# Some twenty operations of a written order change places: cosformer attention with a feed-forward network on one core

## The chip, the core and the metric

The kernel runs on one core of a Trainium2 chip. A core has five engines with a queue of instructions each: TensorE (PE, the matrix products), VectorE (DVE), ScalarE (ACT), GpSimd (POOL) and SyncE (SP), which here only starts DMA transfers. An engine takes its instructions strictly in the order of its queue; between engines semaphores tell that an operand is ready or a buffer is free. The metric is the device time of one execution in microseconds (us), lower is better.

## The reference

Queries, keys and values have 8 batches, 8 heads, 576 positions and 64 columns. The attention has no softmax: relu(q) and relu(k) are multiplied by the cosine and the sine of the position, which gives 128 features each, and so a 128x64 matrix per head takes the place of the matrix of scores.

```python
q_p = concat(relu(q) * cos, relu(q) * sin)      # k_p likewise
kv  = einsum('bhsf,bhsd->bhfd', k_p, v)
z   = sum(k_p, axis=2)
x   = einsum('bhsf,bhfd->bhsd', q_p, kv) / (einsum('bhsf,bhf->bhs', q_p, z) + 1e-06)
h   = x.reshape(4608, 512) @ w_in               # 512 x 2048
g   = maximum(0.01 * h, h)
out = g @ w_out                                 # 2048 x 512, float32
```

## The kernel before

**Groups.** The 4608 rows of x are cut into nine groups of 512 rows. Groups 0 to 7 are the first 512 positions of a batch; group 8 gathers the last 64 positions of all eight. For each batch the features of k are made (nine slices j of 64 positions), then the sum kv over all 576 positions. For each group the features of q are made and transposed by a DMA; numerator and denominator are products with kv on TensorE; DVE divides (`xs`); x is transposed by a DMA (`xT`), and the two products of the feed-forward network follow.

**Products as seven block products.** The first product from group 3 on and the second from group 1 on are cut into 2x2 blocks and each is worked out with seven block products in place of eight, at the price of sums of blocks, which run on DVE and POOL.

**The order is written by hand.** A string, `PROGRAM` (line 25 on), holds 1126 calls such as `k_sin(2,7,D)`; lines 1192 and 1193 parse it and run each call, and every engine executes its instructions in the order in which these calls emit them. Nothing reorders them later, and the waits between engines follow from the data. A call that stands earlier in the string is thus earlier only in the queues of the engines on which it puts instructions. The last letter of an argument list names the engine: D is DVE, A is ACT, P is POOL. The calls that matter here:

- `k_cos(b,j,engine)`, `k_sin(b,j,engine)`: one half of the features of slice j of batch b, a single instruction (line 395 on ACT, line 397 on DVE and POOL) from the staged `kst` into the tile `kp`, of which there is one: a new batch's k operations wait for the kv sum of the batch ahead.
- `kv_sum(b,...)`: 72 small matmuls (line 472) that read the whole `kp` and the values `vm`, and a copy on ACT (line 479).
- `num(b,j)`: 8 matmuls (line 559), and on DVE denominator, reciprocal and product (lines 570, 574, 575) into `xs`.
- `q_prep(b,j,engine)`: two instructions (line 395 or 397) into `qp`; `q_transpose_dma` and `x_transpose_dma` put one DMA each on SP's queue (line 523 for x); `x_sum(b,n,engine)` adds blocks of `xT` into `X` (line 686).
- `M(g,m)`: 128 columns of the first product for all rows of group 1 or 2 (line 633), after each second one a leaky relu on ACT (line 644). After m=15 it also emits two sums of blocks of `g` on DVE.
- `P(g,u,n)`: a block product of the first matrix in groups from 3 on, 4 matmuls of 256 columns (line 786) into one of four PSUM banks `ps_f`. Each unit u uses three banks A, E, B_. `e(g,u,x)` are the operations between them: b copies A to B_, s copies E to `s5`, u copies B_ to `u1` (on ACT, line 403; written as capitals on DVE, line 405), y adds `s5` to B_, z adds `u1` to E (DVE), and a, c, d, e are the leaky relus of the finished blocks (ACT, line 813). P(g,u,7) accumulates onto B_, and so waits until u has copied it.
- `F(g,i)`: 4 matmuls of a block product of the second matrix (line 903) into a bank `ps`; `g_sum(g,n,...)` forms the sums of blocks that products 3, 5 and 6 read (line 686 on DVE). Finished blocks are combined on DVE (line 686) or copied by ACT (lines 922, 931).

Names: `kp<-kst,sin_t` is a k operation, `ext<-g` and `ext<-ext,g` are sums of g, `osb` is a piece of the output on its way to memory, `w_` and `T` are sums of weights.

Of the kernel before, what the change touches and what calls it, by code (L numbers as in the profile page):

```python
# [52 lines left out]
F(1,8) k_sin(3,0,P) k_sin(3,4,P) k_cos(3,0,A) k_cos(3,3,P) k_sin(3,5,D) k_cos(3,5,P) num(2,0)  # L53
q_prep(3,0,0,8,A) k_cos(3,2,A) load(v,3,2,4) F(1,9) q_prep(3,1,0,8,A) F(1,10) F(1,11) F(1,12) num(2,1)
x_transpose(2,0,A) F(1,13) k_cos(3,1,P) F(1,14) k_sin(3,8,P) k_cos(3,4,A) k_sin(3,3,D) k_cos(3,8,P) F(1,15)
v_pairs(3,2,4,P) q_transpose_dma(3,0) k_cos(3,7,A) q_prep(3,3,0,8,A) k_cos(3,6,D) num(2,2) x_transpose(2,1,A)
# [24 lines left out]
g_sum(3,2,4,8,2) P(4,1,1) g_sum(3,1,0,4,1) e(4,0,e) e(4,0,y) e(4,1,b) P(4,1,5) g_sum(3,2,0,4,1)
kv_sum(5,0,4,n) e(4,1,S) P(4,1,2) e(4,1,a) q_transpose_dma(5,1) P(4,1,6) e(4,0,c) F(3,4) x_sum(4,4,D)
g_sum(3,3,5,8,2) q_prep(6,0,0,8,P) load(v,6) num(5,0) F(3,5) P(4,0,4) e(4,1,u) P(4,1,3) e(4,0,d) k_cos(6,2,A)
P(4,1,7) P(4,2,5) g_sum(3,3,0,4,1) e(4,1,z) k_sin(6,6,P) g_sum(3,3,4,8,2) q_prep(6,1,0,8,D) k_sin(6,1,P)
e(4,1,e) F(3,6) F(3,7) k_cos(6,3,P) P(4,2,1) e(4,2,b) F(3,8) e(4,1,y) F(3,9) F(3,10) F(3,11) k_cos(6,4,P)
g_sum(3,4,0,4) num(5,2) e(4,2,s) P(4,1,4) P(4,2,6) k_cos(6,6,A) k_sin(6,2,P) e(4,1,c) F(3,12) e(4,1,d) F(3,13)
num(5,1) P(4,2,3) P(4,2,2) e(4,2,u) e(4,2,z) k_cos(6,7,P) q_transpose_dma(6,0) e(4,2,a) k_sin(6,3,D) P(4,3,1)
F(3,14) k_cos(6,1,A) num(5,3) P(4,2,7) e(4,2,e) e(4,3,b) e(4,2,y) F(3,15) P(4,3,5) P(4,3,6) q_prep(6,2,0,8,P)
q_prep(6,3,0,8,A) e(4,3,s) e(4,2,c) F(3,16) e(4,3,U) F(3,17) k_sin(6,0,D) F(3,18) x_transpose_dma(5)
k_sin(6,7,A) F(3,19) k_cos(6,0,D) P(4,3,7) k_cos(6,5,D) v_pairs(6,0,2,A) k_sin(6,4,D) g_sum(4,1,4,8,2)  # L90
# [1133 lines left out]
```

## Time and profile before

| what | value |
|---|---|
| device time, median of 3 runs | 273.83 us (273.3 to 273.92) |
| device time of the profiled execution | 273.75 us |
| its span, first to last instruction | 272.0 us |
| mean granted TensorE clock | 0.999 |
| PE busy | 264.0 us, 97% |
| DVE busy | 205.9 us, 76% |
| ACT busy | 179.0 us, 66% |
| POOL busy | 132.2 us, 49% |

The profiled execution lies 0.08 us below the median, and 1.75 us of its time lie outside the span. Busy times of matmuls overlap: a row such as `0.60 ... x4` says that 4 matmuls took 0.60 us from the first start to the last end, while the next four start 0.44 us after them. Whether TensorE lost time therefore isn't read from its busy share, but from the starts: the start of one row, plus its matmuls times the pitch at which they follow one another, is when the next row could have started.

### The profile page before, as it was taken

Reading aid. Unit: us, or ns where it says so; the run is one execution under the profiler, and the core shown is the slowest. Engines: PE = TensorE matmul, PEld = TensorE weight load, DVE = VectorE, ACT = ScalarE, POOL = GpSimd, SP = SyncE. Lnnn points to the kernel's source line nnn. Section 1 sums busy time; section 2 is a strip of 40 time slices with the busy share of each in tenths; the row PEclk is TensorE's granted clock in tenths of the full one; section 3 lists DMA queues with packets and bytes.
Section 4 is the critical chain, followed back from the end, with each engine's and each line's share of the span. In section 5 each row is a group of like instructions: output and inputs, shape, how many; then the busy total and the mean of one; then the engine's idle time right before and its main releaser. Section 6 shows DMA issues by size and latency. Waiting matters only on the chain.

```text
span 272.0 us, 7061 instructions
## 1 busy us (share of the span) xinstructions
PE 264.0 (97%) x2877; PEld 218.4 (80%) x2877; DVE 205.9 (76%) x419; ACT 179.0 (66%) x311; POOL 132.2 (49%) x104
## 2 busy tenths in 40 slices
...
GB/s 227 364 395 412 381 398 372 376 296 250 290 200 316 181 216 367 258 91 268 232 224 194 249 363 100 140 214 74 119 154 118 2 116 76 43 41 39 80 39 117
DMA packets 75040, 57.07 MB, mean 210 GB/s; under 512 B 47232, under 2 KB 63616, under 8 KB 74624
## 3 DMA queue, kind: packets, MB, share of 16 engines
...
q14 instruction: 10, 0.08, 0.1%
...
## 4 chain that ended last, share of the span: by engine, by line
PE 88%; DVE 3%; DMA 3%; issue 1%; POOL 1%; ACT 1%; SPq 1%; DVEq 0%; ACTq 0%
PE ps L903 32%; PE ps_f L786 26%; PE ps_h L633 15%; PE ps_o L660 5%; DMA kst<-in_k_dram 3%; PE ps_kv L472 3%; PE ps_num L559 3%; PE ps_f L903 1%; POOL kp L397 1%; PE ps_kv L1003 1%; PE ps_xT L1076 1%; ACT kp L395 1%; PE ps_qt L545 1%; DVE ps_f L686 1%; PE ps_numh L1054 1%
## 5 line engine op out<-in xcount | busy, mean ns | idle before, releaser
L903 PEld LDWEIGHTS <-g 128*128 128x128 f16 x640 | 61.7, 98 | 7.0 <-ACT g L644 0.2
L903 PE MATMUL ps<-w,g 128*128 128x256 f16 x496 | 65.2, 273 | 0.0
L813 ACT ACTIVATE g<-ps_f 128x512 f16<-128x512 f32 x72 | 41.9, 597 | 19.8 <-PE ps_f L786 10.1
L633 PE MATMUL ps_h<-xT,w 128*128 128x512 f16 (+1 forms) x208 | 43.5, 363 | 0.0
L786 PEld LDWEIGHTS <-w 128*128 128x128 f16 x384 | 41.6, 114 | 1.1 <-issue 0.3
L786 PE MATMUL ps_f<-xT,w 128*128 128x256 f16 x288 | 42.1, 273 | 0.2 <-DVE u L405 0.2
L633 PEld LDWEIGHTS <-w 128*128 128x128 f16 x208 | 22.7, 114 | 16.2
L397 POOL TENSOR_SCALAR kp<-kst,cos_t 128x256 f16<-128x256 f32 (+1 forms) x23 | 31.5, 1375 | 4.6 <-DMA kst<-in_k_dram 4.6
L644 ACT ACTIVATE g<-ps_h 128x1024 f16<-128x1024 f32 x24 | 24.1, 1023 | 13.1 <-PE ps_h L633 13.1
L903 PE MATMUL ps<-T,ext 128*128 128x256 f16 x240 | 32.3, 273 | 0.0
L786 PEld LDWEIGHTS <-wext 128*128 128x128 f16 x288 | 31.2, 114 | 0.9 <-issue 0.2
L903 PEld LDWEIGHTS <-ext 128*128 128x128 f16 x256 | 24.8, 98 | 2.6
L397 POOL TENSOR_SCALAR qp<-qst,cos_t 128x512 f16<-128x512 f32 (+1 forms) x10 | 19.4, 1941 | 8.9 <-DMA qst<-in_q_dram 7.5
L397 POOL TENSOR_SCALAR kp<-kst,sin_t 128x256 f16<-128x256 f32 x15 | 21.0, 1402 | 4.5 <-PE ps_kv L472 2.7
L786 PE MATMUL ps_f<-X,wext 128*128 128x256 f16 x144 | 21.5, 273 | 0.0
L686 DVE TENSOR_TENSOR osb<-ps,ext 128x512 f32<-128x512 f32 x23 | 15.8, 689 | 7.3 <-PE ps L903 6.4
L686 DVE TENSOR_TENSOR ps_f<-ps_f,u 128x512 f32<-128x512 f32 x24 | 16.6, 694 | 5.5 <-PE ps_f L786 3.2
L575 DVE TENSOR_TENSOR xs<-ps_num,rden 128x512 f16<-128x512 f32 x28 | 19.4, 692 | 1.0
L813 ACT ACTIVATE g<-y 128x512 f16<-128x512 f32 x24 | 15.2, 632 | 6.9 <-DVE y L686 6.6
L397 POOL TENSOR_SCALAR qp<-qst,sin_t 128x512 f16<-128x512 f32 (+1 forms) x10 | 19.4, 1936 | 0.0
L686 DVE TENSOR_TENSOR ext<-g 128x512 f16<-128x512 f16 (+1 forms) x24 | 14.2, 593 | 4.5 <-ACT g L644 2.8
L686 DVE TENSOR_TENSOR y<-ps_f,s 128x512 f32<-128x512 f32 x24 | 16.4, 684 | 1.4 <-PE ps_f L786 1.3
...
## 6 DMA issues: line engine op xcount, KB each, us to landing
...
```

Source lines behind the costliest of these rows:

```text
L395: nc.scalar.activation(o, i, AF.Relu, scale=col)
L397: eng.tensor_scalar(out=o, in0=i, scalar1=0.0, scalar2=col, op0=ALU.max, op1=ALU.mult)
L472: nc.tensor.matmul(ps[:, o, (c - lo) * NE : (c - lo + 1) * NE], lhsT=st["kp", b][sl, c, j, :], rhs=vm[sl, c, j, :], start=(j == 0), stop=( ...
L559: nc.tensor.matmul(ps[lo:hi, h // 4, (h % 4) * NE : (h % 4 + 1) * NE], lhsT=qpT[:, h, lo:hi], rhs=kv[b][:, h, :],)
L575: nc.vector.tensor_tensor(out=xs, in0=ps[:, :, 0 : 4 * NE].rearrange("p a (b e) -> p a b e", e=NE)[:, :, :, 0:D], in1=rden.rearrange("p (a ...
L633: nc.tensor.matmul(ps[:, m % 2, lo:hi], lhsT=w1[m // 4, c][0][:, w1[m // 4, c][1], m % 4 : 512 : 4], rhs=xT[:, lo // P : hi // P, c, :], s ...
L644: nc.scalar.activation(st["g", g][:, m - 1 : m + 1, :], ps, AF.Lrelu)
L660: nc.tensor.matmul(st["ps_o", g, tt], lhsT=st["g", g][:, m, tt * P : (tt + 1) * P], rhs=w2[:, m, :], start=(m == 0), stop=(m == NFT - 1),)
L686: eng.tensor_tensor(out=o, in0=a, in1=b, op=op)
L786: nc.tensor.matmul(ps[:, mi * HT : (mi + 1) * HT], lhsT=a[:, c, 2 * r0 + mi : 512 : 4], rhs=b[:, c], start=(n in (1, 5) and mi == 0 and c ...
L813: nc.scalar.activation(st["g", g][:, m : m + 2, r * HT : (r + 1) * HT], {"a": A, "c": y22, "e": E, "d": B_}[e].rearrange("p (m t) -> p m t ...
L903: nc.tensor.matmul(ps[:, tt], lhsT=a[:, i, tt * P : (tt + 1) * P], rhs=b[:, i], start=(first and i == 4 * halves[0]), stop=(i == NPR - 1 a ...
```

## The change

No call is added or removed, and each engine gets the same instructions. The string is written with some calls in other places, in six spots; the order on SP's queue is the same. (The new string has one line more, so line 397 of before is line 398 of after, and so on.)

1. Batch 2, k operations (lines 47 to 52). `k_sin(2,6,A)` goes ahead of the last leaky relu of group 1 on ACT. The five k operations of DVE go ahead of `M(1,15)`, and so ahead of the two sums that it emits. `F(1,4)` goes to just behind `F(1,0)`, and `g_sum(1,2,4,6)` ahead of `g_sum(1,3,6,8)`. As before, 28 matmuls of F stand between `M(1,15)` and `kv_sum(2)`.
2. Batch 4: `k_cos(4,0,P)` ahead of `k_sin(4,3,P)` on POOL; `F(2,9)` goes from ahead of `kv_sum(4)` to behind it.
3. Batch 4 and 5: `F(2,15)` goes behind `num(4,2)`, `q_prep(5,1)` behind `q_prep(5,3)`; so on DVE the division of `num(4,2)`, the last before `x_transpose_dma(4)`, comes ahead of three instructions. On POOL `k_sin(5,0)` goes behind `x_sum(4,1)`.
4. Batch 6: `F(3,22)` ahead of `F(3,21)` and `kv_sum(6)`.
5. `k_cos(7,4,D)` behind the copy `e(5,3,U)` on DVE.
6. `e(6,2,s)` behind `e(6,2,b)` on ACT.

The diff, cut to these places (the lines between them hold the same calls, wrapped elsewhere):

```diff
-g_sum(1,1,0,4) M(1,13) q_transpose_dma(2,0) g_sum(1,1,4,6) weight_sum(2) M(1,14) g_sum(1,3,0,6) weight_sum(4)
-M(1,15) F(1,0) k_sin(2,6,A) k_cos(2,3,P) k_cos(2,6,P) k_sin(2,7,D) k_cos(2,4,D) k_sin(2,2,D) k_cos(2,2,P)
-k_sin(2,0,D) k_cos(2,0,A) q_transpose_dma(2,1) k_sin(2,5,P) k_sin(2,3,D) k_cos(2,7,P) k_sin(2,8,P)
-k_cos(2,5,P) k_sin(2,4,A) k_cos(2,1,A) k_sin(2,1,A) F(1,2) F(1,1) g_sum(1,2,0,4) store_held() k_cos(2,8,P)
-F(1,3) g_sum(1,3,6,8) g_sum(1,2,4,6) load(q,4) F(1,4) q_prep(3,2,0,8,A) F(1,5) F(1,6) kv_sum(2,0,4,n) F(1,7)
...
+g_sum(1,1,0,4) M(1,13) q_transpose_dma(2,0) g_sum(1,1,4,6) weight_sum(2) M(1,14) k_sin(2,6,A) g_sum(1,3,0,6)
+weight_sum(4) k_sin(2,7,D) k_cos(2,4,D) k_sin(2,2,D) k_sin(2,0,D) k_sin(2,3,D) M(1,15) F(1,0) k_cos(2,3,P)
+k_cos(2,6,P) k_cos(2,2,P) k_cos(2,0,A) q_transpose_dma(2,1) F(1,4) k_sin(2,5,P) k_cos(2,7,P) k_sin(2,8,P)
+k_cos(2,5,P) k_sin(2,4,A) k_cos(2,1,A) k_sin(2,1,A) F(1,2) F(1,1) g_sum(1,2,0,4) store_held() g_sum(1,2,4,6)
+k_cos(2,8,P) F(1,3) g_sum(1,3,6,8) load(q,4) q_prep(3,2,0,8,A) F(1,5) F(1,6) kv_sum(2,0,4,n) F(1,7) F(1,8)
...
-P(3,0,4) k_sin(4,3,P) k_sin(4,6,A) k_cos(4,0,P) F(2,8) e(3,0,d) P(3,1,2) e(3,1,s) e(3,1,a) P(3,1,6) e(3,1,U)
-F(2,9) kv_sum(4,0,4,n) P(3,1,3) P(3,1,7) e(3,1,z) e(3,0,c) e(3,1,e) num(4,0) F(2,10) w1_sum(1,3,D) F(2,11)
...
+k_cos(4,0,P) P(3,0,4) k_sin(4,3,P) k_sin(4,6,A) F(2,8) e(3,0,d) P(3,1,2) e(3,1,s) e(3,1,a) P(3,1,6) e(3,1,U)
+kv_sum(4,0,4,n) P(3,1,3) F(2,9) P(3,1,7) e(3,1,z) e(3,0,c) e(3,1,e) num(4,0) F(2,10) w1_sum(1,3,D) F(2,11)
...
-e(3,1,c) e(3,2,u) e(3,2,z) e(3,2,a) load(q,6) P(3,2,7) e(3,1,d) e(3,2,y) k_sin(5,5,A) F(2,15) k_cos(5,2,A)
-q_prep(5,2,0,8,P) F(2,16) e(3,2,e) k_cos(5,8,A) q_prep(5,1,0,8,D) P(3,3,1) num(4,2) q_prep(5,3,0,8,D) P(3,3,5)
-k_cos(5,5,P) F(2,17) e(3,3,b) x_transpose_dma(4) q_transpose_dma(5,0) v_pairs(5,2,4,A) P(3,3,6) k_sin(5,0,P)
-F(2,18) P(3,3,2) g_sum(2,4,0,4) e(3,3,s) e(3,3,u) k_cos(5,7,A) P(3,2,4) e(3,2,c) P(3,3,3) x_sum(4,1,P) F(2,19)
...
+e(3,1,c) e(3,2,u) e(3,2,z) e(3,2,a) load(q,6) P(3,2,7) e(3,1,d) e(3,2,y) k_sin(5,5,A) k_cos(5,2,A)
+q_prep(5,2,0,8,P) F(2,16) e(3,2,e) k_cos(5,8,A) P(3,3,1) num(4,2) q_prep(5,3,0,8,D) F(2,15) P(3,3,5)
+k_cos(5,5,P) q_prep(5,1,0,8,D) F(2,17) e(3,3,b) x_transpose_dma(4) q_transpose_dma(5,0) v_pairs(5,2,4,A)
+P(3,3,6) F(2,18) P(3,3,2) g_sum(2,4,0,4) e(3,3,s) e(3,3,u) k_cos(5,7,A) P(3,2,4) e(3,2,c) P(3,3,3)
+x_sum(4,1,P) F(2,19) g_sum(2,4,4,8) F(2,20) k_sin(5,4,P) k_cos(5,0,A) v_pairs(5,0,2,A) P(3,3,7) e(3,3,a)
...
-q_transpose_dma(6,1) k_sin(6,8,D) e(4,3,y) g_sum(3,4,4,8) F(3,21) kv_sum(6,0,4,n) P(4,3,4) load(k,7)
-g_sum(4,2,4,8,2) x_sum(5,1,D) e(4,3,a) g_sum(4,1,0,4,1) F(3,22) x_sum(5,3,P) F(3,23) F(3,24) e(4,3,z) F(3,25)
...
+v_pairs(6,2,4,A) k_sin(6,5,P) e(4,2,d) P(4,3,2) F(3,22) q_transpose_dma(6,1) k_sin(6,8,D) e(4,3,y)
+g_sum(3,4,4,8) F(3,21) kv_sum(6,0,4,n) P(4,3,4) load(k,7) g_sum(4,2,4,8,2) x_sum(5,1,D) e(4,3,a)
+g_sum(4,1,0,4,1) x_sum(5,3,P) F(3,23) F(3,24) e(4,3,z) F(3,25) F(3,26) e(4,3,c) e(4,3,e) e(4,3,d) F(3,27)
...
-q_prep(7,3,0,8,P) e(5,2,e) F(4,15) e(5,3,b) x_transpose_dma(6) g_sum(4,4,4,8) k_cos(7,4,D) F(4,16) e(5,2,c)
-e(5,3,s) P(5,3,6) F(4,17) F(4,18) P(5,2,4) k_cos(7,2,P) k_sin(7,4,P) v_pairs(7,2,4,A) k_cos(7,7,P)
-k_cos(7,3,P) P(5,3,2) v_pairs(7,0,2,P) k_sin(7,7,A) e(5,3,U) g_sum(4,4,0,4) F(4,19) P(5,3,7) load_qtail(0)
...
+e(5,3,b) x_transpose_dma(6) g_sum(4,4,4,8) F(4,16) e(5,2,c) e(5,3,s) P(5,3,6) F(4,17) F(4,18) P(5,2,4)
+k_cos(7,2,P) k_sin(7,4,P) v_pairs(7,2,4,A) k_cos(7,7,P) k_cos(7,3,P) P(5,3,2) v_pairs(7,0,2,P) k_sin(7,7,A)
+e(5,3,U) k_cos(7,4,D) g_sum(4,4,0,4) F(4,19) P(5,3,7) load_qtail(0) k_cos(7,5,A) k_sin(7,6,A) k_cos(7,6,P)
...
-e(6,1,z) g_sum(5,3,0,4,1) F(5,7) e(6,1,a) e(6,1,e) e(6,1,y) P(6,2,5) F(5,8) e(6,0,d) e(6,2,s) num(7,1) F(5,9)
-P(6,2,1) F(5,10) P(6,1,4) q_transpose_dma(8,0) g_sum(5,3,4,8,2) e(6,2,b) P(6,2,6) e(6,1,d) g_sum(5,3,5,8,2)
...
+e(6,1,a) e(6,1,e) e(6,1,y) P(6,2,5) F(5,8) e(6,0,d) num(7,1) F(5,9) P(6,2,1) F(5,10) P(6,1,4)
+q_transpose_dma(8,0) g_sum(5,3,4,8,2) e(6,2,b) e(6,2,s) P(6,2,6) e(6,1,d) g_sum(5,3,5,8,2) num(7,2) e(6,2,u)
```

DVE's queue at the k operations of batch 2, before:

```order
L686 TENSOR_TENSOR g<-g 128x6x256
L686 TENSOR_TENSOR ext<-w_106,T_179 128x2048
L686 TENSOR_TENSOR ext<-g 128x512
L686 TENSOR_TENSOR ext<-ext,g 128x512
L397 TENSOR_SCALAR kp<-kst,sin_t 128x4x64
L397 TENSOR_SCALAR kp<-kst,cos_t 128x4x64
L397 TENSOR_SCALAR kp<-kst,sin_t 128x4x64 x3
L686 TENSOR_TENSOR ext<-ext,g 128x1024
L686 TENSOR_TENSOR g<-g 128x2x256
L686 TENSOR_TENSOR ext<-ext,g 128x512
L686 TENSOR_TENSOR osb<-ps_1034,ext 128x512
```

and after:

```order
L687 TENSOR_TENSOR g<-g 128x6x256
L687 TENSOR_TENSOR ext<-w_106,T_179 128x2048
L398 TENSOR_SCALAR kp<-kst,sin_t 128x4x64
L398 TENSOR_SCALAR kp<-kst,cos_t 128x4x64
L398 TENSOR_SCALAR kp<-kst,sin_t 128x4x64 x3
L687 TENSOR_TENSOR ext<-g 128x512
L687 TENSOR_TENSOR ext<-ext,g 128x512
L687 TENSOR_TENSOR ext<-ext,g 128x1024
L687 TENSOR_TENSOR ext<-ext,g 128x512
L687 TENSOR_TENSOR g<-g 128x2x256
L687 TENSOR_TENSOR osb<-ps_1004,ext 128x512
```

The five `kp` rows now stand ahead of the two sums of 512 columns that `M(1,15)` emits, and the sum of 512 columns ahead of `g<-g`.

DVE's queue around `num(4,2)`, whose division is the rows den, rden and xs, before:

```order
L686 TENSOR_TENSOR y_186<-ps_f_1607,s_185 128x512
L686 TENSOR_TENSOR ext<-ps_1644,ext 128x512
L397 TENSOR_SCALAR qp<-qst,cos_t 128x8x64
L397 TENSOR_SCALAR qp<-qst,sin_t 128x8x64
L570 TENSOR_SCALAR den<-ps_num 128x8
L574 RECIPROCAL rden<-den 128x8
L575 TENSOR_TENSOR xs<-ps_num,rden 128x512
L397 TENSOR_SCALAR qp<-qst,cos_t 128x8x64
L397 TENSOR_SCALAR qp<-qst,sin_t 128x8x64
```

and after:

```order
L687 TENSOR_TENSOR y_186<-ps_f_1607,s_185 128x512
L571 TENSOR_SCALAR den<-ps_num 128x8
L575 RECIPROCAL rden<-den 128x8
L576 TENSOR_TENSOR xs<-ps_num,rden 128x512
L398 TENSOR_SCALAR qp<-qst,cos_t 128x8x64
L398 TENSOR_SCALAR qp<-qst,sin_t 128x8x64
L687 TENSOR_TENSOR ext<-ps_1644,ext 128x512
L398 TENSOR_SCALAR qp<-qst,cos_t 128x8x64
L398 TENSOR_SCALAR qp<-qst,sin_t 128x8x64
```

The three rows up to `xs` have moved ahead of the combination `ext<-ps_1644,ext` and of a pair of q operations.

DVE's queue at the copy into u of unit 3 of group 5, before:

```order
L686 TENSOR_TENSOR ext<-ps_2697,ext 128x512
L686 TENSOR_TENSOR g<-g,ext 128x4x256
L397 TENSOR_SCALAR kp<-kst,cos_t 128x4x64
L405 COPY u_184<-ps_f_1610 128x512
L686 TENSOR_TENSOR g<-g,ext 128x4x256
```

and after:

```order
L687 TENSOR_TENSOR ext<-ps_2697,ext 128x512
L687 TENSOR_TENSOR g<-g,ext 128x4x256
L406 COPY u_184<-ps_f_1610 128x512
L398 TENSOR_SCALAR kp<-kst,cos_t 128x4x64
L687 TENSOR_TENSOR g<-g,ext 128x4x256
```

The k operation has moved one place back, behind the copy.

More of the change, by code (lines that the diff above doesn't have):

```diff
@@ L52 @@
-F(1,3) g_sum(1,3,6,8) g_sum(1,2,4,6) load(q,4) F(1,4) q_prep(3,2,0,8,A) F(1,5) F(1,6) kv_sum(2,0,4,n) F(1,7)
[L53 to L56, printed above, removed]
@@ L81 @@
[L81 to L85, printed above, removed]
@@ L86 @@
[L86 to L90, printed above, removed]
@@ new lines @@
+k_sin(5,3,A) k_sin(5,7,P) e(4,0,z) F(3,3) g_sum(3,2,4,8,2) P(4,1,1) g_sum(3,1,0,4,1) e(4,0,e) e(4,0,y)
+e(4,1,b) P(4,1,5) g_sum(3,2,0,4,1) kv_sum(5,0,4,n) e(4,1,S) P(4,1,2) e(4,1,a) q_transpose_dma(5,1) P(4,1,6)
+e(4,0,c) F(3,4) x_sum(4,4,D) g_sum(3,3,5,8,2) q_prep(6,0,0,8,P) load(v,6) num(5,0) F(3,5) P(4,0,4) e(4,1,u)
+P(4,1,3) e(4,0,d) k_cos(6,2,A) P(4,1,7) P(4,2,5) g_sum(3,3,0,4,1) e(4,1,z) k_sin(6,6,P) g_sum(3,3,4,8,2)
+q_prep(6,1,0,8,D) k_sin(6,1,P) e(4,1,e) F(3,6) F(3,7) k_cos(6,3,P) P(4,2,1) e(4,2,b) F(3,8) e(4,1,y) F(3,9)
```

64 lines of the change are left out of this document (36 added, 28 removed).

## The prediction

> **What bounds the kernel now.** I read the page's first part, then the chain of work that ended last, then TensorE's timeline.
>
> ```profile
> PE 264.0 (97%) x2877; PEld 218.4 (80%) x2877; DVE 205.9 (76%) x419; ACT 179.0 (66%) x311; POOL 132.2 (49%) x104
> ...
> PE 88%; DVE 3%; DMA 3%; issue 1%; POOL 1%; ACT 1%; SPq 1%; DVEq 0%; ACTq 0%
> ```
>
> TensorE is busy for 97% of the span and carries 88% of the chain. A change of order can only win the moments in which it stands still, and lose others.
>
> Busy times of matmuls reach into the gaps behind them and hide a part of them, so I go by starts. The pitch comes from 16 matmuls without a gap, in the first two rows of this timeline of TensorE (start, us, instruction):
>
> ```profile
> 120.97 1.91 PE L903 MATMUL ps<-w,g 128*128 128x256 f16 x16
> 122.72 0.60 PE L786 MATMUL ps_f<-X,w 128*128 128x256 f16 x4
> 123.16 0.60 PE L786 MATMUL ps_f<-xT,w 128*128 128x256 f16 x4
> 123.59 0.60 PE L903 MATMUL ps<-w,g 128*128 128x256 f16 x4
> 124.14 0.60 PE L786 MATMUL ps_f<-X,wext 128*128 128x256 f16 x4
> ```
>
> (122.72 - 120.97) / 16 = 0.109 us, 0.437 for four. Such starts show four places near the change at which TensorE loses time. The last two rows are the smallest: 123.59 + 0.437 = 124.03, the next four start at 124.14, 0.11 late.
>
> **Place 1, the kv sum of batch 2.** TensorE, then DVE, ACT and POOL:
>
> ```profile
> 63.89 3.31 PE L903 MATMUL ps<-w,g 128*128 128x256 f16 x28
> 67.65 1.40 PE L472 MATMUL ps_kv<-vm,kp 64*128 64x66 f16 x72 [0.45 <-ACT ext L922]
> 68.98 0.61 PE L903 MATMUL ps<-w,g 128*128 128x256 f16 x4
> ...
> 77.89 0.60 PE L903 MATMUL ps<-ext,g 128*128 128x256 f16 x4
> 78.43 1.32 PE L472 MATMUL ps_kv<-vm,kp 64*128 64x66 f16 x72
> 79.68 0.62 PE L633 MATMUL ps_h<-xT,w 128*128 128x512 f16 x2
> ```
>
> ```profile
> 65.39 0.61 DVE L686 TENSOR_TENSOR ext<-g 128x512 f16<-128x512 f16 x1
> ...
> 66.37 0.35 DVE L397 TENSOR_SCALAR kp<-kst,sin_t 128x256 f16<-128x256 f32 x1
> ...
> 66.90 0.87 DVE L397 TENSOR_SCALAR kp<-kst,sin_t 128x256 f16<-128x256 f32 x3
> 67.69 0.69 DVE L686 TENSOR_TENSOR ext<-ext,g 128x1024 f16<-128x1024 f16 x1
> ...
> 64.09 1.02 ACT L644 ACTIVATE g<-ps_h 128x1024 f16<-128x1024 f32 x1 [0.70 <-PE ps_h L633]
> ...
> 66.61 0.50 ACT L395 ACTIVATE kp<-kst,sin_t 128x256 f16<-128x256 f32 x1
> ...
> 61.73 4.65 POOL L397 TENSOR_SCALAR kp<-kst,cos_t 128x256 f16<-128x256 f32 x2
> ```
>
> The 28 matmuls of F could end at 63.89 + 28 x 0.109 = 66.94; the kv sum starts at 67.65, 0.71 later. An undisturbed kv sum starts 78.43 - (77.89 + 0.437) = 0.10 late, so about 0.61 is a true stall, and the block that follows is stretched a little (1.33 us from 67.65 to 68.98, against 1.25 from 78.43 to 79.68). The bracket (idle time and what ended it) names ACT's copy `ext`, but a kv sum reads `kp`: POOL's last k operation ended at 61.73 + 4.65 = 66.38, ACT's at 66.61 + 0.50 = 67.11, DVE's five run from 66.37 to 66.90 + 0.87 = 67.77. DVE is the last one.
>
> The change puts DVE's five ahead of the two sums of M(1,15). They then start at 65.39, when DVE is free, and take the 67.69 - 66.37 = 1.32 us that they take now: 66.71. ACT's first k operation fits into the 0.70 us that it idles ahead of the leaky relu at 64.09 (0.50 long), so ACT's last ends one operation earlier, at about 66.6 to 66.7. POOL's order among the k operations hardly matters, since its last ends at 66.38. All are then ready ahead of 66.94. Gain: 0.61, and of the stretched block some 0.04; I take **0.65**, with ends of 0 (the k operations are no earlier, below) and 0.79 (0.71 and the whole 0.08 by which 1.33 exceeds 1.25).
>
> What is late next: the two sums and the sum of 1024 columns slip. All of DVE's work here is the same, so the sum of 1024 columns still ends near 67.69 + 0.69 = 68.38, and the product that reads it stands behind the kv sum and four matmuls, now about 66.94 + 0.10 + 1.25 + 0.44 = 68.73. That leaves 0.3 us, where it had 1.0. F(1,4) reads a finished bank of g and opens an own PSUM bank, so it waits for nothing.
>
> **Place 2, x_sum(4,1) on POOL.** The matmuls at 124.14 read the X that POOL makes:
>
> ```profile
> 115.03 0.42 PE L559 MATMUL ps_num<-kv,qpT 128*128 128x66 f16 x8
> ...
> 116.24 0.16 DVE L570 TENSOR_SCALAR den<-ps_num 128x8 f32<-128x8 f32 x1
> ...
> 116.67 0.69 DVE L575 TENSOR_TENSOR xs<-ps_num,rden 128x512 f16<-128x512 f32 x1
> ...
> 122.93 1.16 POOL L686 TENSOR_TENSOR X<-xT 128x512 f16<-128x512 f16 x1 [1.64 <-DMA xT<-xs]
> ...
> 125.36 1.56 POOL L397 TENSOR_SCALAR kp<-kst,sin_t 128x256 f16<-128x256 f32 x1
> ...
> 128.61 0.56 PE L472 MATMUL ps_kv<-vm,kp 64*128 64x66 f16 x24
> ```
>
> ```profile
> DMA to landing us min/median/max: 4.2/4.6/5.4
> ```
>
> POOL waited for the transposed x, which comes from the last xs, ready at 116.67 + 0.69 = 117.36. The six transposes of x took 4.2 to 5.4 us to land. The eight matmuls of num(4,2) at 115.03 now come four matmuls earlier, at 114.59, and take 0.42. The denominator, which stood at 116.24 behind a combination and a pair of q operations, then starts at about 115.0, and xs ends the same 117.36 - 116.24 = 1.12 us after that, at 116.1, some 1.2 earlier. With the longest transpose, 5.4, x lands at 121.6, where POOL saw it at 122.93, and X is done at 122.8. TensorE, 0.65 ahead, wants X at 124.03 - 0.65 = 123.4. Gain **0.10** (ends 0 and 0.11). More important: the first product of the group, the row of 123.16, reads xT itself. POOL saw xT at 122.93, so it has only some 0.2 us to spare now. Without the earlier transpose, most of place 1's gain would end there. The combination and the q operations come later on DVE: what reads the one on DVE is behind it in any case, and the bank that it frees is written again several units on; the q operations only feed a transpose for the next group. POOL's k_sin(5,0) now follows X: X at 122.8 and three k operations of 1.3 to 1.56 give 127.2 at the most, and the kv sum of batch 5 wants them at 128.61 - 0.75 = 127.9. Hidden, with 0.7 us.
>
> **Places 3 and 4, the two copies.** TensorE and DVE at unit 3 of group 5, TensorE and ACT at unit 2 of group 6:
>
> ```profile
> 171.77 0.60 PE L903 MATMUL ps<-T,ext 128*128 128x256 f16 x4
> 172.56 0.60 PE L786 MATMUL ps_f<-xT,w 128*128 128x256 f16 x4 [0.19 <-DVE u L405]
> ...
> 171.34 0.56 DVE L397 TENSOR_SCALAR kp<-kst,cos_t 128x256 f16<-128x256 f32 x1
> 171.83 0.68 DVE L405 COPY u<-ps_f 128x512 f32<-128x512 f32 x1
> ...
> 189.73 0.60 PE L786 MATMUL ps_f<-xT,w 128*128 128x256 f16 x4
> ...
> 190.60 0.60 PE L786 MATMUL ps_f<-X,w 128*128 128x256 f16 x4
> 191.25 0.60 PE L786 MATMUL ps_f<-X,wext 128*128 128x256 f16 x4
> ...
> 190.12 0.58 ACT L403 COPY s<-ps_f 128x512 f32<-128x512 f32 x1 [1.18 <-DVE den L570]
> 190.60 0.59 ACT L403 COPY ps_f<-ps_f 128x512 f32<-128x512 f32 x1
> ```
>
> Place 3: 171.77 + 0.437 = 172.21, the next start is 172.56: 0.35 lost, until 0.73 after the copy's start at 171.83. With the k operation behind it, the copy starts at 171.34 and lets TensorE go on at 172.07, ahead of 172.21. Gain **0.35** (ends 0 and 0.35). The k operation is for a batch whose kv sum is far off, and the sum behind both ends when it does now.
>
> Place 4: 190.60 + 0.437 = 191.04 against 191.25: 0.21 lost. The copy of A to B_ (190.60) waits behind the copy into s. Its operand, of the matmuls at 189.73, is there at about 190.33 to 190.4; from then it takes the 191.25 - 190.60 = 0.65 that it takes now: 190.98 to 191.05. Gain **0.20** (ends 0.1 and 0.21). The copy into s then starts some 0.8 us later; the addition that reads it comes several units on.
>
> **The rest.** k_cos(4,0) ahead of k_sin(4,3) on POOL: the same two durations, nothing. The kv sum of batch 4 comes four matmuls earlier; TensorE doesn't wait for its k operations now. If they are only just in time, up to 0.44 is lost, otherwise nothing, and F(2,9) fills the same time behind it; I take nothing. F(3,22) ahead of F(3,21): the kv sum of batch 6 comes 0.437 later, its operands wait longer for it; nothing.
>
> **Sum.** 0.65 + 0.10 + 0.35 + 0.20 = 1.30. TensorE being ahead by that much eats small reserves elsewhere (place 1 left 0.3 us where there was 1.0); I take off 0.07, between none and the 0.44 just named, nearer to none since four of the five reserves looked at here hold. The profiled execution's 273.75 becomes 272.5; the median of the runs is 0.08 higher, so **272.6 us**.
>
> **A rule against it.** At place 1 DVE's k operations move under POOL's. Here the rows of both engines show two kinds of meeting, first DVE and POOL with q operations of the same form as the k operations, then with a sum:
>
> ```profile
> 115.85 0.48 DVE L397 TENSOR_SCALAR qp<-qst,sin_t 128x512 f16<-128x512 f32 x1
> ...
> 114.84 1.99 POOL L397 TENSOR_SCALAR qp<-qst,cos_t 128x512 f16<-128x512 f32 x1
> ...
> 169.96 1.46 DVE L686 TENSOR_TENSOR g<-g,ext 128x1024 f16<-128x1024 f16 x1
> ...
> 169.73 1.14 POOL L405 CAST vm<-vst 128x1152 f16<-128x1152 f32 x1
> ```
>
> The sum took 1.46 us, where the row at 67.69 of the same size took 0.69: it seems to have stood until POOL ended at 170.87. The q operation ran from 115.85 to 116.33, wholly inside POOL's 114.84 to 116.83. So a sum is held up by POOL, a q operation, and by its form a k operation, isn't. The Trainium skill, page "SBUF — State Buffer", section "SBUF: two separate sides", says that DVE and GpSimd share a pair of ports as an exclusive lock, for DVE operations in a two-port mode or with two inputs in SBUF: whichever starts first holds it for its whole instruction, and the other fully blocks. The row of 169.96, with two inputs, agrees with it; by the row of 115.85 a q operation doesn't fall under it. If it did, the sum would be 0.65, not 1.30.
>
> **Rivals.**
> (a) Only part arrives. What happened to the sum at 169.96 happens to the k operations at 65.39: they stand until POOL ends at 66.38 and then take 1.32 us, to 67.70, where they end now, and place 1 gains nothing: 0.10 + 0.35 + 0.20 = 0.65, time 273.2. (The port lock of the page above would do this if a k operation took both ports.) Or the transpose of group 4 lands no earlier than now: POOL's X then ends where it does now, and nothing of places 1 and 2 is left behind it: 0.55, time 273.3. For it: the row of 169.96, and that 5.4 us is only the longest of six. Against it: the q operations inside POOL's, and an xs that comes 1.2 us earlier.
> (b) No change: what is put behind each copy and each k operation is wanted as soon as they are, on a DVE busy for 76%, and the stalls return a few steps on. Against it: at places 3 and 4 nothing that moves back is read by the next units. Time 273.8.
> (c) Slower: the transpose of x, now issued at about 116.1, meets other transfers and lands late. TensorE's wait for X then costs every us in full. X ends 1.2 us after the landing; it ends later than now, at 124.14, if x lands after 122.9; the 0.55 of places 3 and 4 is used up at 123.5, and the time is measurably longer from a landing at 124.0, which is 7.9 us after the issue. A transpose of 8.5 us gives 273.8 + 0.6 + 0.5 = 274.9. Against it: 4.2 to 5.4 us in six cases.
>
> **Chances.** Within 0.2% (0.55 us) a measurement of this kernel can't tell a change from none. The forecast has 0.62, with an own range of 272.3 to 272.9 (0.2 us from the ends of the terms of places 1 and 4 and the reserves). (a) has 0.20, with 273.1 to 273.4; about two thirds of it lie beyond 0.2%. (b) 0.10, (c) 0.08. So faster 0.62 + 0.13 = 0.75, same 0.07 + 0.10 = 0.17, slower 0.08. The range goes from 272.2 to 273.4, which leaves out (b) and (c).
>
> **What would show it.** In the profile of after: the kv sum of batch 2 starts at about 67.0 with no wait named, the five k operations start near 65.4 and take 1.3 us; if they start near 66.4, (a) is right. The x transpose of group 4 lands near 121.6 or earlier, and POOL's X is done before TensorE asks. The four matmuls behind the copy into u start 0.44 after the ones ahead, and so do those behind the copy of A to B_. TensorE's last matmul lies 1.2 us earlier against the span's start. The prediction is wrong if a wait of TensorE stands in the list that isn't there now, above all one for xT or for a sum of g.

## The result

| | before | after |
|---|---|---|
| median, 20 runs each | 273.51 us | 272.73 us |
| lowest and highest | 273.17 to 274.21 | 272.26 to 273.83 |
| span of the profiled execution | 272.0 us | 271.0 us |

The ratio of the times is 0.9976, with a 95% interval of 0.9966 to 0.9986: a gain of 0.66 us by the ratio (0.38 to 0.93), 0.78 us by the medians. The time lies within 0.15 us of the forecast 272.6, but that is in part luck: the 20 runs of before have a median 0.3 us below that of the three from which the forecast started. Of the gain of 1.23 us, between half and two thirds came.

The page after the change, first part and chain:

```profile
PE 263.6 (97%) x2877; PEld 218.5 (81%) x2877; DVE 206.6 (76%) x419; ACT 178.8 (66%) x311; POOL 129.3 (48%) x104
...
PE 92%; DMA 3%; POOL 1%; SPq 1%; DVE 1%; issue 0%
```

TensorE carries 92% of the chain, where it carried 88%; DVE and ACT have all but left it. The four places follow, first TensorE's timeline (start, us, instruction; all lines of the code are one higher than before):

```profile
64.36 3.22 PE L904 MATMUL ps<-w,g 128*128 128x256 f16 x28
67.51 1.32 PE L473 MATMUL ps_kv<-vm,kp 64*128 64x66 f16 x72
...
123.36 0.60 PE L904 MATMUL ps<-w,g 128*128 128x256 f16 x4
123.80 0.60 PE L787 MATMUL ps_f<-X,wext 128*128 128x256 f16 x4
...
171.44 0.60 PE L904 MATMUL ps<-T,ext 128*128 128x256 f16 x4
171.88 0.60 PE L787 MATMUL ps_f<-xT,w 128*128 128x256 f16 x4
...
189.92 0.60 PE L787 MATMUL ps_f<-X,w 128*128 128x256 f16 x4
190.36 0.60 PE L787 MATMUL ps_f<-X,wext 128*128 128x256 f16 x4
```

The kv sum of batch 2 starts 67.51 - (64.36 + 28 x 0.109) = 0.10 late, the ordinary amount. At the other three places four matmuls follow four at 0.44. All four stalls are gone. What moved on the other engines, in DVE's, ACT's and POOL's timelines after:

```profile
65.65 0.35 DVE L398 TENSOR_SCALAR kp<-kst,sin_t 128x256 f16<-128x256 f32 x1
...
66.17 0.88 DVE L398 TENSOR_SCALAR kp<-kst,sin_t 128x256 f16<-128x256 f32 x3
...
115.27 0.69 DVE L576 TENSOR_TENSOR xs<-ps_num,rden 128x512 f16<-128x512 f32 x1
115.88 0.88 DVE L398 TENSOR_SCALAR qp<-qst,cos_t 128x512 f16<-128x512 f32 x1
...
171.02 0.68 DVE L406 COPY u<-ps_f 128x512 f32<-128x512 f32 x1
171.62 0.34 DVE L398 TENSOR_SCALAR kp<-kst,cos_t 128x256 f16<-128x256 f32 x1
...
189.74 0.57 ACT L404 COPY ps_f<-ps_f 128x512 f32<-128x512 f32 x1 [1.48 <-PE ps_f L787]
190.22 0.60 ACT L404 COPY s<-ps_f 128x512 f32<-128x512 f32 x1
...
115.79 1.99 POOL L398 TENSOR_SCALAR qp<-qst,sin_t 128x512 f16<-128x512 f32 x1
...
122.07 1.16 POOL L687 TENSOR_TENSOR X<-xT 128x512 f16<-128x512 f16 x1 [1.99 <-DMA xT<-xs]
```

DVE's k operations end at 67.05 and TensorE could go on at 67.41. The last xs is ready at 115.96, 1.4 us earlier than before, and x lands at 122.07.

**How time lost by TensorE is counted below.** From the start of a matmul the pitches of all matmuls ahead of it are taken (0.109 us for 256 columns, 0.216 for 512, 0.032 for a numerator's, 1.25/72 for a kv sum's). What is left grows wherever TensorE stands still. From 62 us on it grows by 2.00 us in the profiled execution of before and by 0.64 in that of after: 1.36 us less, the forecast sum of 1.30. But the span is only 1.0 us shorter, since the start of the F matmuls has moved from 63.89 to 64.36. That 0.47 us arises in the first 20 us, which no moved call touches. Numerator matmuls there in before and in after:

```profile
12.26 0.67 PE L1054 MATMUL ps_numh<-kv,qpT 128*128 128x66 f16 x16 [0.47 <-ACT kv L403]
```

```profile
12.59 0.67 PE L1055 MATMUL ps_numh<-kv,qpT 128*128 128x66 f16 x16 [0.71 <-ACT kv L404]
```

So the first question for the experiments is whether the 1.36 us of one pair of profiles are what the change is worth.

### The profile page after: what moved, and what is told of

Same layout as the page of the kernel before. It is cut to its first block, busy times and chain, and to the rows that moved or that the text cites. A ratio compares the mean times of both kernels' runs of the same rounds, so it can differ in the third digit from the quotient of the medians.

```text
span 271.0 us, 7060 instructions
## 1 busy us (share of the span) xinstructions
PE 263.6 (97%) x2877; PEld 218.5 (81%) x2877; DVE 206.6 (76%) x419; ACT 178.8 (66%) x311; POOL 129.3 (48%) x104
## 4 chain that ended last, share of the span: by engine, by line
PE 92%; DMA 3%; POOL 1%; SPq 1%; DVE 1%; issue 0%
PE ps L904 35%; PE ps_f L787 27%; PE ps_h L634 15%; PE ps_o L661 5%; DMA kst<-in_k_dram 3%; PE ps_num L560 3%; PE ps_kv L473 3%; PE ps_f L904 1%; POOL kp L398 1%; PE ps_kv L1004 1%; PE ps_xT L1077 1%; PE ps_qt L546 1%; PE ps_numh L1055 1%; SPq L274 0%; SPq L260 0%; PE ps_x L536 0%
## 5 line engine op out<-in xcount | busy, mean ns | idle before, releaser
L398 POOL TENSOR_SCALAR kp<-kst,cos_t 128x256 f16<-128x256 f32 (+1 forms) x23 | 30.4, 1328 | 5.0 <-DMA kst<-in_k_dram 5.0
L398 POOL TENSOR_SCALAR kp<-kst,sin_t 128x256 f16<-128x256 f32 x15 | 18.7, 1249 | 2.3 <-PE ps_kv L473 2.3
```

What stands on the lines that cost most here:

```text
L398: eng.tensor_scalar(out=o, in0=i, scalar1=0.0, scalar2=col, op0=ALU.max, op1=ALU.mult)
```

## The experiments

The theory that I held after the result (A in the expectations): the four stalls have fixed sizes and are gone for good, and the rest is start-up. Against it first (B): some stalls come back from execution to execution. After the first four runs another took its place (C): the sizes of the stalls *before* vary between executions of one kernel, as they hang on which of POOL and DVE starts first where they meet. The table has the growth of TensorE's lost time by place, in us, for each profiled execution, before, after and in the order of the runs below; "*" marks a place whose order is the changed one.

| execution | at 50 us | kv sum 2 (62 to 72) | X (112 to 127) | u (160 to 175) | A to B_ (186 to 195) | 62 to 265 us |
|---|---|---|---|---|---|---|
| before | 6.26 | 0.79 | 0.12 | 0.34 | 0.21 | 2.00 |
| after | 6.72 | * 0.10 | * 0.01 | * 0.00 | * 0.00 | 0.64 |
| again | 6.60 | * 0.11 | * 0.02 | * 0.00 | * 0.00 | 0.63 |
| only1 | 6.39 | * 0.19 | 0.02 | 0.36 | 0.00 | 1.10 |
| only3 | 7.58 | 0.67 | * 0.00 | 0.35 | 0.00 | 1.55 |
| only56 | 6.88 | 0.38 | 0.19 | * 0.00 | * 0.00 | 1.09 |
| before_b | 6.47 | 0.59 | 0.02 | 0.00 | 0.00 | 1.14 |
| before_c | 6.35 | 0.62 | 0.03 | 0.36 | 0.00 | 1.52 |
| only1d | 6.31 | 0.27 | 0.18 | 0.34 | 0.00 | 1.40 |
| relief | 6.41 | 0.39 | 0.11 | 0.34 | 0.00 | 1.37 |
| cast_late | 6.38 | 0.83 | 0.06 | 0.00 | 0.00 | 1.41 |
| no3 | 6.49 | * 0.11 | 0.68 | * 0.00 | * 0.00 | 1.30 |

(About 0.10 of the first place is the ordinary loss at a kv sum. The last column also has 0.5 to 0.6 us that all executions share, mostly 0.1 at each later kv sum. The kernels from `before_b` on were timed in one run each, 273.12 to 273.40 us, beside single runs of before at 274.53 and 273.51; such times can't tell tenths apart, so what these kernels show is read from their traces alone.)

### The change again, and its parts alone

`again` emits the instructions of the changed kernel; there is no edit.

> The changed kernel once more, in code that emits the same instructions. Theory A (each of the four stalls is gone for good, and what is missing from the forecast 1.23 us lies in the first 20 us, where the profiled execution after the change had TensorE 0.46 us later than the one before, and which no moved call touches): from the first matmul past 55 us to the end TensorE is again 1.3 to 1.4 us shorter than before, whatever the start-up took, and the time is 0.6 to 1.3 us below before, as the start-up falls. Theory B (some stalls come back from execution to execution): the part past 55 us is shorter by clearly less than 1.3 us, with a gap of over 0.05 us at one of the four places.

Measured: 272.66 us (before beside it 273.61), ratio 0.9964 (0.9952 to 0.9976). Past 62 us it lost 0.63 us, as in the first profile of after, with no gap at any place. B isn't borne out: in none of the executions with the new order at a place does its stall come back. At the copy from A to B_ that says little, since there the old order too lost nothing in most executions, as the next runs show.

`only1` has the calls of batch 2 alone:

```diff
- M(1,15) F(1,0) k_sin(2,6,A) ... k_sin(2,7,D) k_cos(2,4,D) k_sin(2,2,D) ... F(1,2) F(1,1) ... F(1,3) ... F(1,4)
+ k_sin(2,6,A) ... k_sin(2,7,D) k_cos(2,4,D) k_sin(2,2,D) ... M(1,15) F(1,0) ... F(1,4) ... F(1,2) F(1,1) ... F(1,3)
```

> Only the calls of batch 2 are moved. Theory A: the kv sum of batch 2 starts without a wait; past 55 us TensorE is 0.65 us ahead until the first product of group 4, where it stands for the transposed x, which lands when it did: 0.3 to 0.45 us of the gain are lost there and the 0.10 of the wait for X grows; what is left at the end is 0.05 to 0.3 us. Rival (xT is no limit): 0.65 us are left at the end.

Measured: 273.12 us, ratio 0.9987 (0.9972 to 1.0003). The kv sum's loss fell to 0.19, and at X nothing was lost (0.02). My expectation for X was wrong here. POOL's X in this execution:

```profile
122.21 1.16 POOL L686 TENSOR_TENSOR X<-xT 128x512 f16<-128x512 f16 x1 [1.39 <-DMA xT<-xs]
```

x landed at 122.21, against 122.93 before. The transposed x isn't a fixed date: num(4,2) is TensorE's own work and xs follows it, so that when TensorE is ahead, the transpose starts earlier too, here at 116.96 in place of 117.43.

`only3` has the calls around num(4,2) alone:

```diff
- F(2,15) ... F(2,16) ... q_prep(5,1,0,8,D) P(3,3,1) num(4,2) q_prep(5,3,0,8,D) P(3,3,5) ... k_sin(5,0,P) ... x_sum(4,1,P)
+ F(2,16) ... P(3,3,1) num(4,2) q_prep(5,3,0,8,D) F(2,15) P(3,3,5) ... q_prep(5,1,0,8,D) ... x_sum(4,1,P) ... k_sin(5,0,P)
```

> Only the calls around num(4,2) and x_sum(4,1) are moved. Theory A: xs of group 4 is done some 1.2 us earlier, x lands at least 0.8 us earlier, the 0.10 us at the product that reads X is gone; the time falls by 0.1 us, which the timing can't tell from nothing (within 0.2%). Rival (the earlier transpose meets other transfers): it lands no earlier and the time is the same or higher.

Measured: 273.44 us, ratio 0.9998 (0.9983 to 1.0013), nothing lost at X. This execution's start-up was the longest of all (7.58). The timeline of its SP queue shows when the transposes of x and, behind them, of q were issued, and POOL's that x landed:

```profile
117.45 1.78 SPq L523 DMA_TRANSPOSE xT<-xs  x1
...
123.53 1.16 POOL L686 TENSOR_TENSOR X<-xT 128x512 f16<-128x512 f16 x1 [2.02 <-DMA xT<-xs]
```

x took 6.1 us. In the changed kernel it also took 6.1 us (issued at 116.02, landed at 122.07); with the old places it took 5.3 to 5.6 (117.43 to 122.80 in `before_b`). Of the 1.4 us by which the transpose starts earlier some 0.5 are thus lost again, and 6.1 us stand in all three executions with the new places; by what, the runs don't show. Counted from the first F matmul (65.22 here, 63.89 before), x landed 0.7 us earlier, a little less than the 0.8 that I expected.

`only56` has the two copies alone:

```diff
- k_cos(7,4,D) ... e(5,3,U)
+ e(5,3,U) k_cos(7,4,D)
- e(6,2,s) ... e(6,2,b)
+ e(6,2,b) e(6,2,s)
```

> Only the two copies (into u at unit 3 of group 5, from A to B_ at unit 2 of group 6) are moved. Theory A: the gaps of 0.35 and 0.21 us are gone, nothing else changes past 55 us, and the time falls by 0.55 us (ratio 0.998). Rival (the reserves of later work swallow it): under 0.3 us.

Measured: 273.11 us, ratio 0.9987 (0.9976 to 0.9997). Both gaps are gone, but the gain by the ratio is 0.36 us. The table gives the reason: in `only1` and `only3`, which have the old order at the copy from A to B_, there was no gap to win there, and in this one the kv sum of batch 2, whose order it doesn't touch, lost 0.38 in place of 0.79. That speaks for C.

### The sizes of the stalls before

`before_b` and `before_c` emit the instructions of the kernel before.

> The kernel before once more, in code that emits the same instructions. In the executions profiled so far that still had the old order at a place, the delay of batch 2's kv sum came to 0.79, 0.67 and 0.38 us (0.10 of it is ordinary), and the gap at the copy from A to B_ was 0.21 once and 0 twice. Theory C (the sizes of both hang on which of POOL and DVE starts first when they meet, and so vary between executions of one kernel): the part past 55 us differs from the 2.0 us of lost time of the first profile by more than 0.1 us; the gap at A to B_ is 0.2 if POOL's q operation starts ahead of DVE's sum of 1024 columns near 187 us (the sum then takes over 1 us) and 0 if behind it (the sum takes 0.68, POOL's operation over 2.4). The gap at the copy into u is 0.35 as before. Theory A (fixed sizes): 0.79, 0.10, 0.35 and 0.21 again.

> The kernel before a third time, with the same expectations as the second: by theory C other sizes at the kv sum of batch 2 (0.35 to 0.8 us) and 0 or 0.2 at A to B_, by the order in which POOL and DVE start; by theory A 0.79, 0.10, 0.35, 0.21.

Measured: 273.12 and 273.40 us in single runs. The same instructions lost 2.00, 1.14 and 1.52 us past 62 us. C holds, A falls. Only in the first profile is there a gap at A to B_, and it stands where the expectation puts it. (In `before_b` POOL's q operation started 0.6 us behind DVE's sum, and neither lost anything.) POOL's q operation and DVE's sum in the first profile of before, in `before_c` and in `only1`:

```profile
187.61 1.99 POOL L397 TENSOR_SCALAR qp<-qtl,cos_t 128x512 f16<-128x512 f32 x1 [7.36 <-DMA qtl<-in_q_dram]
...
187.73 1.10 DVE L686 TENSOR_TENSOR g<-g 128x1024 f16<-128x1024 f16 x1
```

```profile
187.64 2.46 POOL L397 TENSOR_SCALAR qp<-qtl,cos_t 128x512 f16<-128x512 f32 x1 [7.58 <-DVE ps_f L686]
...
187.55 0.68 DVE L686 TENSOR_TENSOR g<-g 128x1024 f16<-128x1024 f16 x1
```

```profile
187.28 2.44 POOL L397 TENSOR_SCALAR qp<-qtl,cos_t 128x512 f16<-128x512 f32 x1 [7.59 <-DVE ps_f L686]
...
187.17 0.68 DVE L686 TENSOR_TENSOR g<-g 128x1024 f16<-128x1024 f16 x1
```

Where POOL started 0.12 us ahead, the sum lost 0.42 us (1.10 for 0.68); where DVE was 0.1 ahead, POOL lost 0.45 (2.44 to 2.46 for 1.99). In the first case the addition y behind the sum is late, with it the copy into s, which may overwrite `s5` only when y has read it (its row in the prediction names the den right behind y), and with that the copy to B_ and TensorE. In the first profile POOL's wait was ended by a DMA's landing, while DVE's work follows TensorE's: the 0.21 us of place 4 were decided by a tenth of a microsecond. In eight executions with the old order the gap was there once.

That the new order takes this gap away is seen from the copy's row: before, it stood behind the copy into s, which waited for DVE; after (189.74 above), TensorE's matmuls end its wait. The same delay never met the new order: the sum took 0.68 to 0.70 us in `after`, `again` and `only56`, and in `no3` 1.00 us, without a gap, where before it had taken 1.10.

One part of the expectation for `before_b` was wrong: the gap at the copy into u was not 0.35 but 0. DVE's sum and POOL's cast in the first profile of before stand in the prediction (169.96 and 169.73); in `before_b`:

```profile
169.86 0.68 DVE L686 TENSOR_TENSOR g<-g,ext 128x1024 f16<-128x1024 f16 x1
170.46 0.58 DVE L397 TENSOR_SCALAR kp<-kst,cos_t 128x256 f16<-128x256 f32 x1
170.96 0.68 DVE L405 COPY u<-ps_f 128x512 f32<-128x512 f32 x1
171.56 1.64 DVE L686 TENSOR_TENSOR g<-g,ext 128x1024 f16<-128x1024 f16 x1
...
169.31 2.25 POOL L397 TENSOR_SCALAR kp<-kst,cos_t 128x256 f16<-128x256 f32 x2
171.52 1.13 POOL L405 CAST vm<-vst 128x1152 f16<-128x1152 f32 x1
```

POOL was 1.8 us late in its queue; its cast met the next sum, not the one ahead of the copy into u. Either sum ends 0.55 us after the end of the cast that it met (169.96 + 1.46 = 171.42 against 170.87; 171.56 + 1.64 = 173.20 against 172.65). Under POOL's k operation at 169.31 the sum ran its 0.68 us; POOL's next one, at 170.43, started 0.04 us ahead of DVE's k operation, which took 0.58 us in place of 0.34, but that made no gap. So at place 3 the k operation ahead of the copy isn't enough for a gap, the cast is needed too. `cast_late` below tests this.

### What made the kv sum of batch 2 late

`only1d` moves DVE's five k operations and nothing else:

```diff
- M(1,15) ... k_sin(2,7,D) k_cos(2,4,D) k_sin(2,2,D) ... k_sin(2,0,D) ... k_sin(2,3,D)
+ k_sin(2,7,D) k_cos(2,4,D) k_sin(2,2,D) k_sin(2,0,D) k_sin(2,3,D) M(1,15)
```

> Of the calls of batch 2 only the five k operations of DVE are moved ahead of M(1,15); ACT's and POOL's k operations, F(1,4) and the sums stay. If DVE alone was late, the kv sum's delay falls to 0.10 to 0.2 us. If ACT's last k operation is late next (it ended at 67.11 where TensorE could go on at 66.94), 0.2 to 0.3 us remain.

Measured: 0.27 us lost, against 0.38 to 0.83 with the old order and 0.10 with the whole change. DVE was the late one, as the forecast had it. What is left is seen in TensorE's timeline:

```profile
63.95 3.31 PE L903 MATMUL ps<-w,g 128*128 128x256 f16 x28
67.19 1.32 PE L472 MATMUL ps_kv<-vm,kp 64*128 64x66 f16 x72
```

The kv sum starts 67.19 - (63.95 + 28 x 0.109) = 0.19 late, 0.09 more than is ordinary. These 0.09 arise inside the F matmuls, which take 3.31 us as before, and 3.22 where F(1,4) stands ahead of F(1,1) (the row of 64.36 after): the last matmul of F(1,1) started at 65.17 before, 0.06 behind the end of ACT's last leaky relu of the group (64.09 + 1.02). The other 0.07 us lie ahead of the first numerator behind the kv sum, which started at 69.40, as ACT's copy of kv had ended at 69.35; with ACT's k operation moved, it costs nothing there. So each of the two calls is worth less than 0.1 us.

`relief` leaves DVE's order as it was and takes two k operations off POOL:

```diff
- k_sin(2,8,P) ... k_cos(2,8,P)
+ k_cos(2,8,A) M(1,13) ... M(1,14) k_sin(2,8,A)
```

> The order before, but two of POOL's k operations of batch 2 are done by ACT instead, in the 0.7 us that it idles ahead of leaky relus; POOL's last k operation then ends 2.3 us or more earlier, ahead of DVE's sums near 64 to 66 us. Theory C: these sums then take 0.95, 1.22 and 0.42 us, as where POOL was done early, and the kv sum's delay is 0.3 to 0.45 us with the k operations of DVE where they were. Theory A (only DVE's order counts): 0.65 to 0.8 us.

Measured: 0.39 us lost, in the expected range. POOL's last k operations of the batch, and DVE from the sums to the k operations:

```profile
59.41 2.49 POOL L397 TENSOR_SCALAR kp<-kst,cos_t 128x256 f16<-128x256 f32 x2
...
63.33 0.95 DVE L686 TENSOR_TENSOR g<-g 128x1536 f16<-128x1536 f16 x1
64.19 1.22 DVE L686 TENSOR_TENSOR ext<-w,T 128x2048 f16<-128x2048 f16 x1
65.33 0.42 DVE L686 TENSOR_TENSOR ext<-g 128x512 f16<-128x512 f16 x1
...
66.65 0.87 DVE L397 TENSOR_SCALAR kp<-kst,sin_t 128x256 f16<-128x256 f32 x3
```

POOL is done at 61.90, where it was at 66.38, and the sums take 0.95, 1.22 and 0.42 us. In the profile of before, with POOL still at work, the sum of 512 columns at 65.39 took 0.61. So about 0.4 us of the 0.79 that were lost there in that profile came from sums that POOL held up (0.79 against 0.39), about 0.2 from DVE's order, 0.09 from the wait of F(1,1), and 0.10 is ordinary. The other executions with the old order agree: against `relief`, DVE's five sums from 61 to 66 us took 0.38 us longer in all in before, 0.25 in `only3`, 0 in `only56`, 0.16 in `before_b`, 0.19 in `before_c` and 0.41 in `cast_late`, and TensorE lost 0.39 us plus that much in each, within 0.04.

### The cast and the copy into u

`cast_late` moves one operation of POOL by one place:

```diff
- v_pairs(7,0,2,P) ... k_cos(7,6,P)
+ k_cos(7,6,P) v_pairs(7,0,2,P)
```

> The order before, but POOL's cast into vm (1152 columns, 1.14 us) goes behind the next k operation on POOL. Nothing moves on DVE or TensorE: k_cos(7,4) is still ahead of the copy into u. Theory C (the 0.35 us at the copy into u come from POOL's cast, which starts 0.2 us ahead of DVE's sum of 1024 columns and holds it up): the sum near 169.9 us takes 0.68 in place of 1.46 us and the gap at the copy into u is 0, as in the second profile of before, in which the cast came late by itself. Rival (any operation of POOL in that place holds the sum up, or the k operation ahead of the copy alone makes the gap): the sum takes over 1 us, or the gap stays at 0.3 us or more.

Measured: no gap at the copy into u (0.00), with k_cos(7,4) still ahead of it. DVE, POOL and TensorE there:

```profile
170.04 0.82 DVE L686 TENSOR_TENSOR g<-g,ext 128x1024 f16<-128x1024 f16 x1
170.78 0.34 DVE L397 TENSOR_SCALAR kp<-kst,cos_t 128x256 f16<-128x256 f32 x1
171.05 0.67 DVE L405 COPY u<-ps_f 128x512 f32<-128x512 f32 x1
...
167.61 3.37 POOL L397 TENSOR_SCALAR kp<-kst,cos_t 128x256 f16<-128x256 f32 x3
170.94 1.19 POOL L405 CAST vm<-vst 128x1152 f16<-128x1152 f32 x1
...
171.85 0.60 PE L903 MATMUL ps<-T,ext 128*128 128x256 f16 x4
172.28 0.60 PE L786 MATMUL ps_f<-xT,w 128*128 128x256 f16 x4
```

The sum took 0.82, a little more than the 0.68 that C expected, under POOL's k operations, and TensorE went on at 172.28 without a gap. The gap thus has two causes, and either can be taken away: the cast of POOL in front of the sum, or the k operation between sum and copy.

### The changed kernel without the calls of num(4,2)

`no3` is the changed kernel with the edit of `only3` undone.

> The changed kernel with the calls around num(4,2) and x_sum(4,1) back in their old places. The gap ahead of the product that reads X is between 0 and 0.2 us, as it was in the profiles with the old places (0.11, 0.19, 0.01, 0.01 and 0.01 us, and 0.17 and 0.10 us in the two single moves of batch 2); nothing else changes past 55 us: 0.65 to 0.85 us lost, where the changed kernel loses 0.64. If what the forecast said held (without the earlier transpose most of the gain of batch 2 ends at the first product of group 4), 0.3 us or more would be lost there.

Measured: 0.68 us lost, nearly all of it at the first product of the group and at the one that reads X:

```profile
122.27 0.60 PE L786 MATMUL ps_f<-X,w 128*128 128x256 f16 x4
123.01 0.63 PE L786 MATMUL ps_f<-xT,w 128*128 128x256 f16 x4
123.47 0.60 PE L903 MATMUL ps<-w,g 128*128 128x256 f16 x4
124.24 0.60 PE L786 MATMUL ps_f<-X,wext 128*128 128x256 f16 x4 [0.17 <-POOL X L686]
```

By the starts 123.01 - (122.27 + 0.437) = 0.30 and 124.24 - (123.47 + 0.437) = 0.33 us. This is the case that the forecast feared, and more than the 0.2 that I had come to expect after `only1`. DVE's and POOL's timelines show why xs was late:

```profile
115.19 0.67 DVE L397 TENSOR_SCALAR qp<-qst,cos_t 128x512 f16<-128x512 f32 x1
115.78 0.90 DVE L397 TENSOR_SCALAR qp<-qst,sin_t 128x512 f16<-128x512 f32 x1
...
117.03 0.69 DVE L575 TENSOR_TENSOR xs<-ps_num,rden 128x512 f16<-128x512 f32 x1
...
115.56 2.15 POOL L397 TENSOR_SCALAR qp<-qst,sin_t 128x512 f16<-128x512 f32 x1
```

The two q operations, which in the old places stand ahead of the division, took 0.67 and 0.90 in place of 0.48, as POOL's q operation started at 115.56, during the first of them. In `only1`, with the same places, xs started at 116.20. So the calls around num(4,2) are worth between 0 and 0.7 us, by the same meeting of two engines, and with the division in front of the q operations the delay falls behind xs, where it costs nothing: after the change the q operation at 115.88 took 0.88 us too.

## Why the prediction was right, and where it was off

**The places and their mechanisms hold.** All four stalls that it read from the starts are gone in both profiles of the changed kernel, by the moves it named, and no new wait took their place. (For the copy from A to B_ this rests on its row, as the old order lost nothing there either in most executions.) The sum of 1.30 us against 1.36 for that one pair of profiles is close. That the time came out only 0.13 us off is in part luck: the forecast gain was 0.45 us above that of the medians, and the time that it was taken from 0.32 us above the median of the 20 runs of before.

**The step that was off is the size of the terms.** Each was read from one execution of before, and that one had lost more than its kind does. Over the executions with the old order at a place, the mean loss was:

- kv sum of batch 2: (0.79 + 0.67 + 0.38 + 0.59 + 0.62 + 0.83) / 6 = 0.65, less the 0.10 that remains: 0.55, where the prediction took 0.65. (`relief` and `only1d`, which change something else there, are left out.) The prediction put all of the stall down to DVE's k operations. It took the 28 matmuls of F at the bare pitch, so that the 0.09 us of F(1,1) stand in its 0.61 as DVE's, and it didn't see that DVE's sums of 63.17 and 65.39, 1.15 and 0.61 us long, were held up by POOL (0.95 and 0.42 in `relief`).
- X: 0.09 in eight executions of an otherwise old or partly changed order, and 0.68 in one; the prediction took 0.10. Its remark that the earlier transpose protects the gain of batch 2 is borne out by `no3` and not by `only1`.
- copy into u: 0.34, 0.36, 0.35, 0.00, 0.36, 0.34, 0.34: 0.30, for the predicted 0.35. (`cast_late`, which moves the cast, is left out.) The prediction named the k operation ahead of the copy; the gap needs POOL's cast too.
- copy from A to B_: 0.21 once and 0 in seven others: 0.03, for the predicted 0.20. This is the term that failed.

The three profiles of before lost 2.00, 1.14 and 1.52 us past 62 us, 1.55 on average, the two of the changed kernel 0.64 and 0.63. The difference of 0.92 us agrees with the 0.78 and 0.95 us of the medians and lies inside both intervals (0.38 to 0.93, and 0.66 to 1.31 from `again`). The 1.36 us of the two profiles shrank to 1.0 in their spans by start-up: at 50 us it lies between 6.26 and 7.58 in the twelve executions, 6.26, 6.47 and 6.35 in the three of before, 6.72 and 6.60 in the two of the changed kernel. Five executions don't tell whether that last difference is more than chance; no moved call lies ahead of 50 us.

**The rivals.** (a), a part only, was near in size but not in cause. Neither are DVE's k operations held up (they start at 65.65 and take 1.31 us) nor is the landing of x the limit in the full change; what was missing had never been there in most executions. The case that would have tested the port lock at place 1 didn't arise in any of the five executions with DVE's k operations in the new place: in the first profile of after POOL was done with its own at 62.69, where it had been at work until 66.38, and in the others at least 0.3 us ahead of DVE's. So that rival is untested there. (b) falls, with an interval of `again` that lies wholly beyond 0.2%, and so does (c), though x took 6.0 us to land with the new places, by the view that gave the prediction its longest of 5.4: (c) goes in that direction, with reserve left.

**The deduction of 0.07** for eaten reserves wasn't needed: between 72 and 112 us and past 127 us the changed order lost what the old one did.

**The rule weighed against the trace.** The prediction concluded from the q operation at 115.85 that q and k operations of DVE aren't held up by POOL. That was too much from one row: started 0.1 to 0.2 us behind POOL's, a q operation took 0.88 us after the change, and 0.90 in `no3`. Nor does it hold for k operations: the one at 170.46 in `before_b` took 0.58 us, and the prediction's own row of 171.34 has 0.56, where 0.34 is usual. The Trainium skill, page "SBUF — State Buffer", section "SBUF: two separate sides", says that DVE and GpSimd have a pair of ports under an exclusive lock, which the first to start holds for its whole instruction. That who starts first wins is what the rows at 187 us show, in both directions; in `after`, where POOL's row starts 0.02 us ahead, POOL lost 0.5 us all the same. That the loser waits for the whole instruction is right for the cast (either sum ended 0.55 us after its end) but not for POOL's q operations of 1.99 us, behind whose start DVE lost 0.32 to 0.42 us, nor for its k operation at 169.31, under which a sum ran its 0.68 us.
